# A list schedule for the engine order, a permutation product for the slot exponentials, and token sums in the experts' mask

## The chip, the cores and the metric

The kernel runs on one core of a Trainium2 chip. The metric is the device time of one execution in microseconds, median of several runs; the profile is one execution of its own, with a span from its first to its last instruction and a somewhat longer measured time. The core has TensorE (PE, with a separate row PEld for its weight loads), VectorE (DVE), ScalarE (ACT), GpSimd (POOL, which here issues the input loads and makes a few constants) and SyncE (SP, which issues the output stores). Each engine works through its own instructions in order.

## The reference

Two stages. The first is causal attention for 4 batches, 8 heads, 768 positions and head dimension 64. Heads marked as retrieval see all earlier positions; the others see the first 4 positions and a window of 64. The result, as 3072 rows of 512, goes into a soft mixture of experts with 8 experts of 4 slots each:

```python
    scores = scale * np.matmul(q, k.transpose(0, 1, 3, 2))
    ...
    stream_keep = causal & (is_sink | in_win)
    ...
    a = np.exp(scores)
    a = a / (np.sum(a, axis=-1, keepdims=True) + 1e-09)
    return np.matmul(a, v).astype(np.float32)
...
    logits = x @ phi
    d = np.exp(logits - logits.max(0)); d /= d.sum(0) + 1e-09
    slot_input = (d.T @ x).reshape(E, S_per_e, D)
    for e in range(E):
        h = np.maximum(slot_input[e] @ w1[e], 0.0)
        slot_out[e] = h @ w2[e]
    c = np.exp(logits - logits.max(1)); c /= c.sum(1) + 1e-09
    return (c @ slot_out).astype(np.float32)
```

(The lines of the second part are shortened; x is the attention's result, w1 is 512 x 1024 for each expert, w2 is 1024 x 512.) The two softmaxes of the second part share their exponentials: one is divided by a sum over tokens for each slot, the other by a sum over slots for each token.

## The kernel before

**Units.** A unit of attention is a pair of heads, number n of 16; two pairs make a quad Q, four pairs a batch b. All matmul operands are bf16; the loads convert from f32. A raw quad of q, k or v holds 16 consecutive tokens in one partition, so that one load is a few long runs. In this layout a block of 128 tokens is a permutation of the natural order.

**One quad's turns.** `turn_half` (L79; `turn_pair`, L90, for quad 0, which arrives in two pieces) transposes half of a quad's q, k or v by 16 TensorE transposes into a PSUM buffer of the pool "tr" (two buffers, L57), and `copy` (L104) brings it to SBUF, by VectorE ("V") or ScalarE ("A"). `turn_back` (L110) transposes v once more into the rows that the second product reads. ScalarE takes the second half of k and of v; VectorE the rest.

**One pair.** `qk` (L134) makes the scores of the causal triangle in six groups of 448 columns for both heads, each into one of two PSUM buffers of the pool "sc" (L55), and ScalarE's exponential (L142) writes each group to pT. `mask` (L145) multiplies parts of pT by 0/1 masks on VectorE; `make_vfar` (L121) makes a masked copy of v for blocks far from the diagonal; `pvmm` (L163) makes the products with v, with a column of ones for the row sums, in one PSUM buffer; `norm` (L175) divides, on VectorE, into xb. `x_transpose` (L186) turns xb through "tr" into xT.

**One batch.** `logits` (L195) multiplies xT by phi in "tr", and ScalarE's exponential (L206) writes el, four times repeated over 128 columns. `exp_slots` (L208) transposes el through "tr", and ScalarE copies it to expT (L214), which is kept for the end, with its sum over tokens in colpart. The copy puts the tokens into natural order by its output pattern: element s of a run of 16 comes 16 elements, 32 bytes, behind its neighbour in the loop that writes. `dispatch` (L230) sums el times xb for the batch in "tr" and adds it to slot_acc (L240). `row_sums` (L221) makes the sums over slots from expT.

**Order.** The loop over n (L404) writes out by hand which group goes to each engine's queue and where: scores of pair n, products of pair n-1 between them, the turns of the next quad as four `tasks`, and the slot work of the last full batch in the four pairs behind it. A PSUM group and the instruction that empties it are issued side by side.

**Loads.** POOL issues them in program order: q, k, v of the next quad but one when the present quad has been turned, the 16 weight loads of 1 MB (as bf16) in between. Their SBUF tiles for w2 of experts 4 to 7 are first used as the raw buffers and the masks, so these loads come last.

**End.** Behind the loop stand the logits of the last batch, `exp_slots`, `dispatch`, the sum over tokens (csum, L510), its reciprocal (rcol, L512), and the scaling of slot_acc to slot_sc (L516). Then sip (L523), its copy siT (L524), two groups of hp against w1 (L535), the relu and mask hs (L539 on ScalarE, L540 on VectorE; emask, made at L399, is 1 where a row belongs to the expert), `second` against w2 (L557), and the output rows with their stores (L582 to L600).

Of the kernel before, what the change touches and what calls it, by code (L numbers as in the profile page):

```python
# [21 lines left out]
UNIT = 448  # L22
# [15 lines left out]

class Attn:
# [3 lines left out]
    def __init__(self, nc, tc, ctx, sctx, src, env):  # L43
# [16 lines left out]
        self.lg, self.el = {}, {}  # L60
# [20 lines left out]
    def turn_half(self, t, Q, hf, eng):  # L81
        raw = self.raws[t][Q % 2]
        tp = self.trp.tile([128, 8, 96], BF16, tag="tr", name="tp" + t)
        for s in range(8):
            d0 = (8 * hf + s) * 64
            for hp in range(2):
                self.nc.tensor.transpose(tp[64 * hp:64 * hp + 64, s, :], raw[:96, hp, d0:d0 + 64],  # L87
                                         self.ident[:96, :96])
        dst = self.blocked(t, Q).rearrange("c g (s p) -> c s g p", p=8)[:, 8 * hf:8 * hf + 8]
        self.copy(eng, dst, tp.rearrange("c s (g p) -> c s g p", p=8))  # L90

    def turn_pair(self, t, a, eng):
        raw = self.raws[t][0]
        p0 = 64 * a
        tp = self.trp.tile([128, 16, 48], BF16, tag="tr", name="tp" + t)
        for s in range(16):
            for hp in range(2):
                self.nc.tensor.transpose(tp[64 * hp:64 * hp + 64, s, :],  # L98
                                         raw[p0:p0 + 48, hp, s * 64:s * 64 + 64],
                                         self.ident[p0:p0 + 48, p0:p0 + 48])  # L100
        dst = self.blocked(t, 0).rearrange("c g (s p) -> c s g p", p=8)[:, :, 6 * a:6 * a + 6]
        self.copy(eng, dst, tp.rearrange("c s (g p) -> c s g p", p=8))

    def copy(self, eng, o, i):  # L104
        if eng == "A":
            self.nc.scalar.copy(o, i)  # L106
        else:
            self.nc.vector.tensor_copy(o, i)  # L108

    def turn_back(self, Q, a, eng):  # L110
        tp = self.trp.tile([128, 6, 2, 64], BF16, tag="tr", name="tpb")
        vT = self.vT[Q]
        for i in range(6):
            self.nc.tensor.transpose(tp[:, i].rearrange("p h d -> p (h d)"), vT[:, 6 * a + i, :],  # L114
                                     self.ident)
        self.copy(eng, self.vbs[Q % 2][:, a, :, :, :64].rearrange("p h j d -> p j h d"), tp)
# [13 lines left out]
    def qk(self, n, u):  # L130
# [4 lines left out]
        for j, q0, o, w in unit_pieces(u):  # L135
            for hh in range(2):
                ps = slice(64 * hh, 64 * hh + 64)
                nc.tensor.matmul(sc[:, hh, o:o + w], kT[ps, (g0 + j) * 128:(g0 + j + 1) * 128],  # L138
                                 qT[ps, g0 * 128 + q0:g0 * 128 + q0 + w], start=True, stop=True)
        if u == 0:  # L140
            self.pT[n] = self.ptp.tile([128, 2, NPT], BF16, tag="pT", name="pT")
        nc.scalar.activation(self.pT[n][:, :, u * UNIT:(u + 1) * UNIT], sc[:, :, :UNIT], ACT.Exp,  # L142
                             scale=self.scale)
# [41 lines left out]
    def x_transpose(self, n):  # L185
# [7 lines left out]
        self.nc.vector.tensor_copy(self.xT[b][:, n4], tp)  # L193

    def logits(self, b, i0, i1):  # L195
# [7 lines left out]
        if i1 == 6:  # L203
            self.el[b] = self.small.tile([128, 6, 4, 32], BF16, tag="el", name="el")
            lg = self.lg[b].rearrange("p i (o s) -> p i o s", o=1)
            nc.scalar.activation(self.el[b], lg.to_broadcast([128, 6, 4, 32]), ACT.Exp)  # L206

    def exp_slots(self, b):  # L208
        nc = self.nc
        tp = self.trp.tile([128, 768], BF16, tag="tr", name="tpe")  # L210
        for i in range(6):
            nc.tensor.transpose(tp[:, i * 128:(i + 1) * 128],  # L212
                                self.el[b][:, i].rearrange("p g s -> p (g s)"), self.ident)
        nc.scalar.activation(self.expT[:, b, :].rearrange("g (i p s) -> g i s p", i=6, p=8),  # L214
                             tp.rearrange("g (i s p) -> g i s p", i=6, p=8), ACT.Copy,
                             accum_out=self.colpart[:, b:b + 1])
# [4 lines left out]
    def row_sums(self, b):  # L221
# [6 lines left out]
        self.nc.vector.reciprocal(self.rrow[:, b, :], rp)  # L228

    def dispatch(self, b):  # L230
        nc = self.nc
        sp = self.trp.tile([128, 512], F32, tag="tr", name="slp")
        for i in range(6):
            g = i % 4
            nc.tensor.matmul(sp[32 * g:32 * (g + 1), :], self.el[b][:, i, 0, :], self.xb[b][:, i, :],
                             start=(i < 4), stop=(i + 4 >= 6))
        if b == 0:
            nc.vector.tensor_copy(self.slot_acc, sp)
        else:
            nc.vector.tensor_add(self.slot_acc, self.slot_acc, sp)  # L240
# [3 lines left out]
def kernel(  # L244
# [34 lines left out]
    phi = singles.tile([P, 4, ES], BF16, name="phi")  # L279
    quarter = singles.tile([P, 1], BF16, name="quarter")  # L280
# [15 lines left out]
    tkf = singles.tile([P, 2], F32, name="tkf")  # L296
# [9 lines left out]
    def w2_half(e, c):  # L306
# [6 lines left out]
               slot_acc=slot_acc, msk=msk, fmask=fmask, scale=1.0 / (D ** 0.5), raws=raws, vbs=vbs)  # L313
# [7 lines left out]
    with tc.tile_pool(name="setup", bufs=1) as setup:  # L321
# [21 lines left out]
        for vb in vbs:  # L343
            nc.vector.memset(vb, 1.0)
        nc.vector.tensor_single_scalar(ident, iti, 0.0, op=ALU.is_equal)
        at.turn_pair("q", 0, "V")
        at.turn_pair("k", 0, "A")
# [6 lines left out]
        nc.vector.tensor_single_scalar(tkf[:, 1:2], tkf[:, 0:1], float(n_sink), op=ALU.is_lt)  # L354
        causal = setup.tile([P, 256], BF16, name="causal")
# [16 lines left out]
    head_mask(0)  # L372
    head_mask(2)
# [3 lines left out]
    def weights(c):  # L377
        for _ in range(c):
# [8 lines left out]
    weights(1)  # L387

    def setup_sums():
        nc.gpsimd.tensor_copy(phi, phf)  # L390
        nc.gpsimd.memset(sum4, 1.0)
        for g in range(4):
            nc.gpsimd.affine_select(sum4[32 * g:32 * (g + 1)], sum4[32 * g:32 * (g + 1)],
                                    pattern=[[-1, ES]], compare_op=ALU.is_equal,
                                    fill=0.0, base=0, channel_multiplier=1)
        for e4 in range(2):
            for g in range(4):
                s0 = SPE * (4 * e4 + g)
                nc.vector.reduce_sum(emask[32 * g:32 * (g + 1), e4:e4 + 1],  # L399
                                     sum4[32 * g:32 * (g + 1), s0:s0 + SPE], axis=AX.X)  # L400

    NWQ = [1, 1, 2, 1, 2, 1]
    none = lambda: None

    for n in range(NP + 1):
        last = n == NP
        Q = n // 2
        tasks = []
        if n == 0:
            tasks = [lambda: at.turn_pair("v", 0, "V"), lambda: at.turn_back(0, 0, "V"),  # L410
                     lambda: at.turn_pair("q", 1, "V"), lambda: at.turn_pair("k", 1, "A")]
        elif n % 2 == 1 and Q + 1 < NQ:
            tasks = [lambda: at.turn_half("q", Q + 1, 0, "V"), lambda: at.turn_half("k", Q + 1, 0, "V"),
                     lambda: at.turn_half("q", Q + 1, 1, "V"), lambda: at.turn_half("k", Q + 1, 1, "A")]
            if n == 1:
                tasks += [lambda: at.turn_pair("v", 1, "V"), lambda: at.turn_back(0, 1, "V")]
        elif n % 2 == 0 and not last:
            tasks = [lambda: at.turn_half("v", Q, 0, "V"), lambda: at.turn_half("v", Q, 1, "A"),
                     lambda: at.turn_back(Q, 0, "V"), lambda: at.turn_back(Q, 1, "V")]
        tasks += [none] * 6  # L420

        def loads():
            if n % 2 == 0 and Q + 2 < NQ:
# [3 lines left out]
            elif n % 2 == 1 and Q + 2 < NQ:  # L427
                at.load("v", Q + 2)
                weights(NWQ[Q] - 1)

        if Q > 0:
            loads()
        if n == 1:
            setup_sums()
        if n == 12:
            weights(12 - wi[0])
        if n == 15:
            w_load(NE + 4)
            w_load(NE + 5)

        b = (n - 5) // 4
        bt = (n - 5) % 4 if n >= 5 else None

        def qk(u):
            if not last:
                at.qk(n, u)

        qk(0)
        tasks[0]()
        if bt == 0:  # L450
            at.logits(b, 0, 3)
        qk(1)
        if n:
            for i in range(5):
                at.pvmm(n - 1, 0, i)
        if bt == 0:
            at.logits(b, 3, 6)
        qk(2)
        if n:
            at.pvmm(n - 1, 0, 5)  # L460
            for i in range(3):
                at.pvmm(n - 1, 1, i)
        if not last:
            at.mask(n, 0, 4)
        qk(3)
        if n:
            for i in range(3, 6):
                at.pvmm(n - 1, 1, i)
            at.norm(n - 1)
        if bt == 0:  # L470
            at.exp_slots(b)
        tasks[1]()
        qk(4)
        tasks[2]()
        if not last:
            at.mask(n, 1, 3)
        if bt == 1:
            at.dispatch(b)
        qk(5)
        tasks[3]()  # L480
        if n:
            at.x_transpose(n - 1)
        if not last:
# [164 lines left out]
```

## Time and profile before

| | |
|---|---|
| median of 3 runs | 198.06 us (197.72 to 199.22) |
| profiled execution: time, span | 196.88 us, 195.2 us |
| mean granted TensorE clock | 0.847 of full speed |
| PE busy, share of the span | 141.5 us, 72% |
| PEld | 93.8 us, 48% |
| VectorE | 117.1 us, 60% |
| ScalarE | 125.4 us, 64% |
| POOL | 30.6 us, 16% |
| POOL's DMA queue | 26.22 MB, its packets took 73.2% of 16 engines' span |
| stage: before the first exponential | 0 to 8.7 us |
| stage: attention loop, first to last exponential | 8.7 to 145.7 us |
| stage: last products to siT | 145.7 to 159.4 us |
| stage: experts and output rows | 159.4 to 186.5 us |
| stage: last stores landing | 186.5 to 195.2 us |

The groups of a page list busy time, the mean of one instruction, and the idle time of its engine just before it with what ended that idle time. A busy TensorE is not one at its peak: at half the granted clock the same work shows as more busy time. In a timeline the duration belongs to the merged run of instructions.

### The profile page before, as it was taken

Reading aid. Unit: us, or ns where it says so; the run is one execution under the profiler, and the core shown is the slowest. Engines: PE = TensorE matmul, PEld = TensorE weight load, DVE = VectorE, ACT = ScalarE, POOL = GpSimd, SP = SyncE. Lnnn points to the kernel's source line nnn. Section 1 sums busy time; section 2 is a strip of 40 time slices with the busy share of each in tenths; the row PEclk is TensorE's granted clock in tenths of the full one; section 3 lists DMA queues with packets and bytes.
Section 4 is the critical chain, followed back from the end, with each engine's and each line's share of the span. In section 5 each row is a group of like instructions: output and inputs, shape, how many; then the busy total and the mean of one; then the engine's idle time right before and its main releaser. Section 6 shows DMA issues by size and latency. Waiting matters only on the chain. (4 is left out here: it accounts for less than half of the span.)

```text
span 195.2 us, 5613 instructions
## 1 busy us (share of the span) xinstructions
PE 141.5 (72%) x2508; PEld 93.8 (48%) x2508; DVE 117.1 (60%) x247; ACT 125.4 (64%) x148; POOL 30.6 (16%) x58
## 2 busy tenths in 40 slices
PE   7888888878939788893997889479674536688500
PEld 2455655655726465672654666346354212475100
DVE  6679987987544769654648867464865222136600
ACT  3376848789896777979765887976670531318620
POOL 7615051032012103200322000021031000000000
PEclk9955969999985999998569999966997558999965
DMA  4999999999989954999799997049969900008997
GB/s 65 169 194 224 202 226 200 225 201 222 212 181 138 220 107 77 200 213 188 113 222 205 212 215 151 3 64 217 187 81 149 168 1 3 0 3 265 342 405 278
DMA packets 16087, 32.93 MB, mean 169 GB/s; under 512 B 1728, under 2 KB 8896, under 8 KB 14272
## 3 DMA queue, kind: packets, MB, share of 16 engines
q0 software_dynamic: 11216, 26.22, 73.2%
q1 hardware_dynamic: 4848, 6.37, 9.3%
q8 instruction: 19, 0.31, 0.6%
q14 instruction: 4, 0.03, 0.0%
HBM read 52.50 MB, written 6.29 MB: 301 GB/s over the span
## 5 line engine op out<-in xcount | busy, mean ns | idle before, releaser
L142 ACT ACTIVATE pT<-sc 128x896 bf16<-128x896 f32 x96 | 86.2, 926 | 27.0 <-PE sc L138 22.9
L161 DVE TENSOR_TENSOR pT<-pT,w 128x1024 bf16<-128x1024 bf16 (+1 forms) x64 | 31.8, 518 | 23.5 <-ACT pT L142 23.5
L138 PE MATMUL sc<-qT,kT 64*128 64x128 bf16 (+4 forms) x352 | 39.5, 302 | 3.3 <-ACT kT L106 2.5
L170 PEld LDWEIGHTS <-pT 128*128 128x128 bf16 x672 | 27.5, 105 | 16.3 <-issue 16.2
L170 PE MATMUL pv<-vf,pT 128*128 128x65 bf16 x320 | 27.1, 205 | 5.0 <-DVE vf L125 4.9
L170 PE MATMUL pv<-vb,pT 128*128 128x65 bf16 x352 | 30.4, 205 | 0.0
L87 PEld LDWEIGHTS <-w 96*64 96x64 bf16 x672 | 20.2, 121 | 19.2 <-issue 18.2
L138 PEld LDWEIGHTS <-kT 64*128 64x128 bf16 x352 | 11.4, 98 | 13.0 <-ACT kT L106 4.1
L182 DVE TENSOR_TENSOR xb<-pv,rs 128x768 bf16<-128x768 f32 x16 | 15.3, 957 | 0.6
L87 PE MATMUL tpq<-ident,w 96*64 96x96 bf16 x224 | 8.2, 220 | 10.2 <-ACT expT L214 9.1
L108 DVE COPY qT<-tpq 128x768 bf16<-128x768 bf16 x16 | 8.8, 552 | 10.3 <-PE tpq L87 7.6
L214 ACT ACTIVATE expT<-tpe 128x768 bf16<-128x768 bf16 x4 | 13.6, 3399 | 0.9 <-PE tpe L212 0.9
L191 PE MATMUL tpx<-ident,xb 128*128 128x128 bf16 x96 | 9.3, 242 | 3.7 <-DVE xb L182 2.0
L114 PE MATMUL tpb<-ident,vT 128*128 128x128 bf16 x96 | 8.4, 226 | 4.6 <-ACT vT L106 4.0
L108 DVE COPY vb<-tpb 128x768 bf16<-128x768 bf16 x16 | 8.9, 554 | 4.9 <-PE tpb L114 4.9
L68 POOL DMA_DIRECT2D w<-in_q_dram x7 | 4.5, 645 | 43.3 <-PE tpq L87 21.8
L125 DVE TENSOR_TENSOR vf<-vb,fmask 128x528 bf16<-128x528 bf16 x16 | 11.1, 695 | 0.0
L193 DVE COPY xT<-tpx 128x768 bf16<-128x768 bf16 x16 | 8.9, 555 | 3.4 <-PE tpx L191 3.0
L106 ACT COPY kT<-tpk 128x768 bf16<-128x768 bf16 x9 | 7.2, 797 | 5.4 <-PE tpk L98 5.2
L114 PEld LDWEIGHTS <-vT 128*128 128x128 bf16 x96 | 5.6, 100 | 8.3 <-ACT vT L106 5.9
L87 PE MATMUL tpk<-ident,w 96*64 96x96 bf16 x224 | 8.1, 219 | 1.9 <-DVE kT L108 1.9
L191 PEld LDWEIGHTS <-xb 128*128 128x128 bf16 x96 | 6.8, 107 | 5.1 <-DVE xb L182 2.4
(89 smaller groups left out, 164.2 us busy)
## 6 DMA issues: line engine op xcount, KB each, us to landing
w<-in_moe_w_dram POOLq DMA_DIRECT2D x14, 1024.0 KB, 13.2
out_dram<-ot SPq DMA_DIRECT2D x12, 256.0 KB, 3.1
out_dram<-ot SPq DMA_DIRECT2D x6, 512.0 KB, 4.9
w<-in_q_dram POOLq DMA_DIRECT2D x7, 384.0 KB, 6.7
w<-in_k_dram POOLq DMA_DIRECT2D x7, 384.0 KB, 7.2
w<-in_v_dram POOLq DMA_DIRECT2D x7, 384.0 KB, 8.9
w<-in_moe_w_dram POOLq DMA_DIRECT2D x4, 512.0 KB, 9.3
w<-in_q_dram POOLq DMA_DIRECT2D x2, 192.0 KB, 5.4
```

What stands on the lines that cost most here:

```text
L87: self.nc.tensor.transpose(tp[64 * hp:64 * hp + 64, s, :], raw[:96, hp, d0:d0 + 64], self.ident[:96, :96])
L108: self.nc.vector.tensor_copy(o, i)
L114: self.nc.tensor.transpose(tp[:, i].rearrange("p h d -> p (h d)"), vT[:, 6 * a + i, :], self.ident)
L125: self.nc.vector.tensor_mul(vf, self.vbs[n // 2 % 2][:, n % 2, :, :4, :], fm.to_broadcast([128, 2, 4, VW]))
L138: nc.tensor.matmul(sc[:, hh, o:o + w], kT[ps, (g0 + j) * 128:(g0 + j + 1) * 128], qT[ps, g0 * 128 + q0:g0 * 128 + q0 + w], start=True, sto ...
L142: nc.scalar.activation(self.pT[n][:, :, u * UNIT:(u + 1) * UNIT], sc[:, :, :UNIT], ACT.Exp, scale=self.scale)
L161: nc.vector.tensor_mul(v, v, m)
L170: self.nc.tensor.matmul(pv[:, hh, i * 65:(i + 1) * 65], pT[:, hh, o:o + 128], (vb if i - j <= 1 else vf)[:, j, :65], start=(j == 0), stop= ...
L182: nc.vector.tensor_mul(x, pv[:, :, :, :64], rs.to_broadcast([128, 2, 6, 64]))
L191: self.nc.tensor.transpose(tp[:, i * 128:(i + 1) * 128], self.xb[b][:, i, n4 * 128:(n4 + 1) * 128], self.ident)
L193: self.nc.vector.tensor_copy(self.xT[b][:, n4], tp)
L214: nc.scalar.activation(self.expT[:, b, :].rearrange("g (i p s) -> g i s p", i=6, p=8), tp.rearrange("g (i s p) -> g i s p", i=6, p=8), ACT ...
```

## The change

1. **Order.** The handwritten loop is replaced by a class `Plan`. It lists every group of instructions as an operation with an engine, a cost, a delay until others see its result, what it depends on, a rank (place in the order of pairs plus an offset by kind), and, for PSUM users, the pool. `order` is a list schedule: it keeps a time for each engine, and takes again and again the operation that could start first; on one engine, among those that could start within `lead`, the lowest rank. TensorE pays 0.115 for a change of row groups. The instructions are then issued in that order. Each PSUM group and the copy that empties it are operations of their own, so the functions are split (`turn`/`turned`, `back`/`blocked_back`, `qk`/`exp`, `x_transpose`/`x_transposed`, and so on). All v turns are copied by VectorE; ScalarE keeps the second half of k.
2. **Slot exponentials.** The transposes in `exp_slots` become matmuls of el with a permutation matrix `perm`, into an "sc" buffer in f32; ScalarE copies it in natural order without a stride.
3. **Token sums.** slot_sc is now slot_acc plus the last batch's dispatch, added directly and not scaled; the reciprocal of the token sums scales emask, which the relu applies. emask's sums move from pair 1 to the end.
4. **Small ones.** Only the last two columns of the v tiles are set to ones; head masks 1 and 3 are made before the loop; weight loads are spread as 1, 1, 1, 1, 1, 2 with the rest behind the turn of v of quad 6 and w2 of experts 4, 5 behind that of quad 7.

The core of the diff:

```diff
+    def turn(self, t, Q, h, deps, rank, at=0.0, cost=0.33):
+        n = f"{t}{Q}.{h}"
+        back = t == "b"
+        self.add("T" + n, "PE", cost, 0.27, deps, rank, "T", mode="F" if back else "C", slot=("tr", "e" + n), at=at)
+        eng = self.evac.get(n, self.evac.get(f"{t}{h}", "DVE"))
+        c, d = (0.68, 0.85) if eng == "ACT" else (0.464, 0.6)
+        self.add("e" + n, eng, c, d, ["T" + n], rank, "eT")
...
+                add(f"Q{n}.{u}", "PE", 0.19, 0.27, d, n + u / 6, "Q", mode="H", slot=("sc", f"x{n}.{u}"))
+                d = [f"Q{n}.{u}"] + ([f"P{n - 2}.1.B"] if u == 0 and n > 1 else [])
+                add(f"x{n}.{u}", "ACT", 0.814, 0.95, d, n + u / 6, "x")
...
+            for h in range(2):
+                d = [f"Tb{Q - 1}.1"]
+                self.turn("v", Q, h, d, n + 1 + h / 4, at=8.0 if Q == 1 else 0.0)
...
+                add(f"G{b}", "PE", 0.35, 0.27, [f"el{b}"], n + 0.4, "G", slot=("sc", f"eG{b}"))
+                add(f"eG{b}", "ACT", 1.2, 1.35, [f"G{b}"], n + 0.5, "eG")
...
+                    st = max(r, free[e])
+                    key = (st if st > free[e] + lead else free[e], o["rank"])
+                    if top is None or key < top[0]:
+                        top = (key, st + (SWITCH if e == "PE" and o["mode"] != mode else 0.0), o)
...
+RANK = {"D": -0.22, "V": 1.15, "x": 2.77, "M": -1.62, "eX": 0.07, "eD": 0.79, "M5": -0.31, "eT": -0.45,
+        "X": 0.66, "P": 0.44, "G": 0.12, "el": -0.31, "L": -0.76, "H": -0.26, "N": -0.18, "eG": 0.8,
+        "T": -0.79}
+EVAC = {"k1": "ACT"}
+LEAD = 0.1
...
     def exp_slots(self, b):
-        tp = self.trp.tile([128, 768], BF16, tag="tr", name="tpe")
+        tp = self.scp.tile([128, 2, 512], F32, tag="sc", name="tpe")
         for i in range(6):
-            nc.tensor.transpose(tp[:, i * 128:(i + 1) * 128],
-                                self.el[b][:, i].rearrange("p g s -> p (g s)"), self.ident)
-        nc.scalar.activation(self.expT[:, b, :].rearrange("g (i p s) -> g i s p", i=6, p=8),
-                             tp.rearrange("g (i s p) -> g i s p", i=6, p=8), ACT.Copy,
-                             accum_out=self.colpart[:, b:b + 1])
+            o = 128 * (i % 3)
+            self.nc.tensor.matmul(tp[:, i // 3, o:o + 128], self.el[b][:, i].rearrange("p g s -> p (g s)"),
+                                  self.perm, start=True, stop=True)
+        self.tp["g", b, 0] = tp
+
+    def exp_slots_out(self, b):
+        self.nc.scalar.activation(self.expT[:, b, :].rearrange("g (a c) -> g a c", a=2),
+                                  self.tp.pop(("g", b, 0))[:, :, :384], ACT.Copy,
+                                  accum_out=self.colpart[:, b:b + 1])
...
-            nc.vector.memset(vb, 1.0)
+            nc.vector.memset(vb[:, :, :, :, 64:], 1.0)
...
+        nc.vector.tensor_tensor(tkf[:, 2:3], tkf[:, 0:1], tk[:, 0:1], op=ALU.subtract)
+        nc.vector.tensor_scalar(perm, iti, tkf[:, 2:3], None, op0=ALU.is_equal)
...
-    head_mask(0)
-    head_mask(2)
+    for h in (0, 2, 1, 3):
+        head_mask(h)
...
+    def after_turn(t, Q):
+        turned.add((t, Q))
+        if Q + 2 < NQ:
+            if t == "v":
+                at.load("v", Q + 2)
+                weights(NWQ[Q] - 1)
+            elif ("q", Q) in turned and ("k", Q) in turned:
+                at.load("q", Q + 2)
+                at.load("k", Q + 2)
+                weights(1)
+        elif t == "v" and Q == NQ - 2:
+            weights(12)
+        elif t == "v":
+            for e in (4, 5):
+                w_load(NE + e)
...
+    at.dispatch(bl)
+    slp = at.tp.pop(("d", bl, 0))
+        nc.vector.tensor_add(slot_sc[:, cs].rearrange("p (h a d) -> p a h d", h=2, a=2),
+                             pair(slot_acc), pair(slp))
     at.exp_slots(bl)
-    at.dispatch(bl)
+    at.exp_slots_out(bl)
+    for e4 in range(2):
+        for g in range(4):
+            s0 = SPE * (4 * e4 + g)
+            nc.vector.reduce_sum(emask[32 * g:32 * (g + 1), e4:e4 + 1],
+                                 sum4[32 * g:32 * (g + 1), s0:s0 + SPE], axis=AX.X)
     csum = at.small.tile([P, 1], F32, tag="cs", name="csum")
     nc.vector.reduce_sum(csum, colpart, axis=AX.X)
     rcol = at.small.tile([P, 1], F32, tag="rc", name="rcol")
     nc.vector.reciprocal(rcol, csum)
-        nc.vector.tensor_scalar_mul(slot_sc[:, cs].rearrange("p (h a d) -> p a h d", h=2, a=2),
-                                    slot_acc[:, cs].rearrange("p (a h d) -> p a h d", h=2, a=2), rcol)
+    nc.vector.tensor_scalar_mul(emask, emask, rcol)
```

## The prediction

> **What bounds the kernel now.** I read the page first, then the exponentials of ScalarE in order of time (one pair of heads is six of them), then TensorE in order of time around the odd gap, then a table of stretches, and last the chain of waits for the end of the kernel.
>
> The page, groups of instructions (busy us, mean ns | idle before, releaser):
>
> ```profile
> L142 ACT ACTIVATE pT<-sc 128x896 bf16<-128x896 f32 x96 | 86.2, 926 | 27.0 <-PE sc L138 22.9
> L87 PE MATMUL tpq<-ident,w 96*64 96x96 bf16 x224 | 8.2, 220 | 10.2 <-ACT expT L214 9.1
> L214 ACT ACTIVATE expT<-tpe 128x768 bf16<-128x768 bf16 x4 | 13.6, 3399 | 0.9 <-PE tpe L212 0.9
> ```
>
> The attention loop runs from the first exponential at 8.71 us to the last one's end at 145.71: 137.0 us, in which ScalarE is idle 27.0 us, mostly for scores. One instruction stands out: the slot copy, 3.40 us, four times.
>
> TensorE in order of time (start, duration, [idle before]):
>
> ```profile
> 52.84 0.53 PE L87 MATMUL tpk<-ident,w 96*64 96x96 bf16 x16
> 53.31 0.37 PE L138 MATMUL sc<-qT,kT 64*128 64x256 bf16 x4
> 56.72 0.64 PE L87 MATMUL tpq<-ident,w 96*64 96x96 bf16 x16 [3.04 <-ACT expT L214]
> 57.29 0.56 PE L138 MATMUL sc<-qT,kT 64*128 64x320 bf16 x4
> 57.77 0.85 PE L87 MATMUL tpk<-ident,w 96*64 96x96 bf16 x16
> ```
>
> TensorE stands 3.04 us because the slot transposes hold one of the two "tr" buffers until the slow copy ends; afterwards the same 16 transposes take 0.85 us, not 0.53. The table of stretches (PE, PEld, DVE, ACT, POOL busy; PEclk; DMA share; GB/s) says why:
>
> ```profile
> 34.00:57.00 23.00, 17.20 (x382) 12.49 (x383) 16.86 (x36) 19.85 (x22) 3.02 (x5) 1.00 1.08 216
> 57.00:64.00 7.00, 6.83 (x97) 4.28 (x91) 3.55 (x8) 4.76 (x6) 1.83 (x3) 0.51 0.86 138
> 64.00:92.00 28.00, 21.27 (x452) 15.20 (x452) 19.39 (x39) 23.31 (x26) 3.66 (x6) 0.98 0.87 168
> 92.00:101.00 9.00, 8.83 (x129) 5.95 (x125) 4.87 (x10) 5.65 (x8) 1.83 (x3) 0.50 0.83 148
> ```
>
> After this wait and its two repetitions (before 91.59 and 127.41, 3.04 us each) the granted clock is 0.50 to 0.54 for 7 to 9 us; elsewhere in the loop from 34 us it is about 1.0.
>
> The chain of waits, at the end (start, duration):
>
> ```profile
> 153.36 0.84 PE tpe L212 x6
> 154.22 3.42 ACT expT L214 x2
> ...
> 158.06 0.63 DVE slot_sc L516 x2
> 158.69 0.05 issue
> 158.73 0.33 PE sip L523 x4
> 159.06 0.02 issue
> 159.08 0.30 DVE siT L524
> ```
>
> Here the fourth copy lies on the path itself. The sum below is made on the span of 195.2 us; the profiled run took 196.88 us, the median of the runs is 198.06, so 2.9 us is added to a span.
>
> **Part 1, the slot copy in the loop.** Starts of the first exponential give the periods of pairs 3 to 14: 7.92, 6.47, 11.90, 8.97, 7.67, 6.33, 12.11, 9.71, 7.67, 6.33, 11.60, 9.46. Undisturbed, an odd pair takes 7.67 and an even one 6.38. Pairs 5, 9, 13 hold the copy: excess 4.23 + 4.44 + 3.93 = 12.6. Pairs 6, 10, 14 hold the half clock: 2.59 + 3.33 + 3.08 = 9.0. Sum 21.6 us. What stays, three times: the exponential of the logits (0.71 us, from its start at 50.96 to the next start at 51.67) and a copy that writes in order. The nearest row for that copy is L206, 128x768 from f32 PSUM, 0.81 us; the accumulator read (0.50 us) overlaps the old copy, so between 0.81 and 1.31: I take 1.2. That is 3 x 1.95 = 5.85. **Gain 15.7 us** (21.6 if the stays fit in ScalarE's idle time; 12.6 - 5.85 = 6.7 if the half clock has another cause than the wait). The product with the permutation is 6 matmuls for 6 transposes, nothing on TensorE. It takes a "sc" buffer: for about 0.4 + 1.2 us the scores have one buffer, so ScalarE may wait one score group (0.30 us) once or twice, up to 1.8 us in three rounds, against the same time freed in "tr"; inside the bound above.
>
> The Trainium skill speaks against the half of this. TensorE: Matmul & The Clock Gate, "What's actually happening", says that the clock falls after a whole idle window of about 3.4 us; 3.04 us would not fill it. By that rule the 9.0 us would have another cause and stay, and the sum below would be 179.2. I go by the rows: three waits of 3.04 us, three falls of the clock directly behind them, and no wait of that length and no fall elsewhere from 34 to 128 us.
>
> **Part 2, the order.** At full clock the three engines have, per pair, from start to start in the timeline: ScalarE 6 exponentials at 0.845 (3.38 for four in a row), one kT copy per two pairs (0.70), slot work 0.49: 5.9. The seven vT copies leave it for VectorE. VectorE: masks 0.60 + 0.60 + 0.53, vf 0.62, norm 1.13, xT 0.47, 3.5 turned copies at 0.47, slot work 0.18: 5.8. TensorE: scores 6 x 0.30 (46.70 to 47.00), pv 1.35 (15 matmuls in 0.48, so 42), turns (6 x 0.46 + 2 x 0.44)/2 = 1.82, x 0.43, slot work (0.92 + 0.42 + 0.55 + 0.16)/4 = 0.51: 5.9. So nothing in the loop can be below 5.9 per pair, and the order of before, with the slot work that stays, makes (7.67 + 6.38)/2 + 0.49 = 7.5. The odd pairs carry four q and k turns and no room for them; spreading these is what a list order can win. Three engines at the same load leave no slack for in-order queues: I take 6.6, nearer the middle than the floor. 12 pairs x 0.9 = **11.0 us gain**; floor 5.9 gives 19.4, the old spacing 0. Pairs 0 to 2 (7.9, 9.6, 7.6; half clock until 18.6 us) I leave, as their clock does not come from the order.
>
> **Small edits.** Two more head masks (1 and 3) stand before the loop: 4 x 0.42 = 1.7 us on VectorE ahead of the first vT copy at 10.78; VectorE is idle 0.3 to 0.9 us at a time there: cost 0.8, between 0 and 1.7. The ones of vb shrink (2 x 1.38 us at 1.5 to 4.5 us), but TensorE runs its zeros until 5.63 and the identity is ready at 4.63: nothing; without the zeros it would be 2.5. Two tiny setup operations, 0.35 us, replace the 1.27 us of emask sums, which go to the end. The loads move on POOL's queue: 26.22 MB at about 215 GB/s are 122 us in all. By the sum below the last exponential ends at 145.7 - 15.7 - 11.0 + 0.8 = 119.8. Four weights (1 MB, 4.9 us each) are issued behind v's turn of quad 6 (about 2 pairs of 6.6 earlier than the last turn), w2 of experts 4 and 5 behind v's turn of quad 7, which is ranked 2.8 pairs before the end (about 101 us), the halves of 6 and 7 behind the last mask (about 121). Four halves of 2.4 us land near 131; second() for experts 6 and 7 begins 13.6 us behind siT (as in the chain of before), near 145. Hidden by 14 us.
>
> **Part 3, the end.** From the end of the exponential of the logits (153.31) to the end of siT (159.38) are 6.07 us. After: dispatch 1.04 (its row at the half clock), two adds from PSUM, about 0.45 each (an estimate from the 0.69 us of the whole add), so the sums are ready at +2.0. TensorE's permutation, 0.82 behind dispatch, is done at +1.9, the copy of 1.2 at +3.2. On VectorE, eight emask sums (1.27 us) stand in the queue, then csum, which waits for the copy, then rcol and the scaling, and behind them siT, which all of hp waits for. csum and rcol follow each other by 0.19 and 0.20 us in the chain of before; so csum starts at 3.2, rcol at 3.4, the scaling at 3.6, siT at 3.8 and ends at +4.1. sip itself is done at +2.4 and is covered. **Gain 2.0 us** (1.0 to 3.6, the latter if nothing stood ahead of siT). The first hp group runs cold (3.59 us against 1.87) and stays so: TensorE is idle here in both. From there the 35.8 us to the end are not changed.
>
> Sum: -15.7 - 11.0 + 0.8 - 2.0 = -27.9; 195.2 - 27.9 = 167.3 span, 198.06 - 27.9 = **170.2 us**.
>
> **Rivals.** (a) The order wins nothing: TensorE's real group times differ from the plan's (it has 0.33 us for 16 transposes, the rows 0.46 start to start, with a separate charge of 0.115 for a change of mode), so a fixed order stalls where the old one did. Then -15.7 + 0.8 - 2.0: 181.2. For it: the three loads are equal. Against: odd pairs at 7.67 with even ones at 6.38 show unevenness that any spreading removes.
> (b) Slower: the clock does not come back. At the half clock a pair costs TensorE 6 x 0.49 + 2.63 (15 pv matmuls in 0.94) + 3.1 (16 transposes in 0.79) + 0.76 + 0.9 (slot work) = 10.4 us; 13 such pairs, from 33.9 us on, and the 49.5 us behind the last exponential, less 2.0, give a span of 33.9 + 135 + 47.5 = 216, or 219 us. It decides from 8.7 us per pair, that is when more than 55% of the pairs run cold. For it: between 22 and 26 us TensorE is idle only 0.39 to 0.65 us at a time, busy 63%, and the clock is 0.57 behind. Against: at 6.6 per pair it would be busy 90%.
> (c) The copy does not get faster: if f32 PSUM or the accumulator made the 3.40 us and not the stride of 32 bytes at the output, part 1 is lost, part 2 halved, and part 3 about zero: 193 us. Against: L206 reads f32 PSUM of the same size in 0.81 us.
>
> **Numbers.** The forecast (both parts) 0.74, 161 to 177; (a) 0.18, 177 to 184; (b) 0.04, 200 and above; (c) 0.04, 188 to 196. The low end 161 is the floor of 5.9 per pair (170.2 - 8.4 = 161.8) with a little of the bound of part 1. The range 161 to 182 leaves out (b), (c) and the upper part of (a). Within 1% is what this measurement can't tell from no change. Half of (c) falls within 1% if its order wins less still. Faster by over 1%: 0.74 + 0.18 + 0.02 = 0.94; same 0.02 from (c); slower 0.04 from (b).
>
> **What would show it.** Part 1: the expT row near 1 us, no 3 us wait of TensorE, PEclk about 1.0 from pair 3 to 15. Part 2: pairs of equal length near 6.6, ScalarE about 90% busy in the loop, the last exponential ending near 120 us. Part 3: the end of siT about 4.1 us behind the exponential of the logits, csum in the chain. Wrong if the PEclk row has fives inside the loop, if "sc" or "tr" waits of 2 us or more come up in TensorE's queue, or if the pairs stay above 7.5.

## The result and the profile after

The changed kernel takes 164.06 us (median of 4 runs, 162.0 to 166.7) against 198.64 us in the same comparison, 34.6 us less; the forecast was 27.9 us less. The ratio is 0.818, with a 95% interval of 0.808 to 0.828. Executions of one kernel spread by 1 to 5 us with the mean clock (0.899 at a span of 160.3 us, 0.862 at 165.0), so every ratio here leaves the slow ones out, and the rows of four profiles below are an upper end (v's copies on ScalarE, both moves of masks, the second set at the start: 2 to 4 us above their fastest). The profiled execution has a span of 160.3 us, 34.9 us less than before. The spans by stage, from the timelines of the two kernels:

| stage | before | after | difference | forecast |
|---|---|---|---|---|
| start to the first exponential of pair 3 | 33.9 | 35.2 | +1.3 | +0.8 |
| pairs 3 to 15, to the end of the last exponential | 111.8 | 79.5 | -32.3 | -26.7 |
| to the end of the last exponential of the logits | 7.6 | 6.0 | -1.6 | 0 |
| from there to the first hp product | 6.1 | 3.7 | -2.4 | -2.0 |
| to the end | 35.8 | 35.8 | 0.0 | 0 |

The page of the changed kernel, groups of instructions (busy us, mean ns, then idle before and its releaser):

```profile
L283 ACT ACTIVATE pT<-sc 128x896 bf16<-128x896 f32 x96 | 81.6, 922 | 9.6 <-PE sc L276 7.8
L302 DVE TENSOR_TENSOR pT<-pT,w 128x1024 bf16<-128x1024 bf16 (+1 forms) x64 | 32.1, 519 | 3.3 <-ACT pT L283 2.7
```

ScalarE waits 9.6 us ahead of its exponentials, where it was 27.0, and VectorE 3.3 us ahead of its masks, where it was 23.5. One exponential is not faster (922 ns, 926 before).

ScalarE in order of time in the changed kernel, around the first slot copy (start, duration):

```profile
54.41 0.81 ACT L362 ACTIVATE expT<-tpe 128x768 bf16<-128x768 f32 x1
55.12 0.19 ACT L362 ACTIVATION_READ_ACCUMULATOR expT<-tpe 128x1 f32 x1
55.21 0.91 ACT L283 ACTIVATE pT<-sc 128x896 bf16<-128x896 f32 x1
```

The copy is 0.81 us in place of 3.40, and from its start to the next exponential it takes 0.80 us: nothing of the accumulator read stands on the path.

The table of stretches of the changed kernel (PE, PEld, DVE, ACT, POOL busy; PEclk; DMA share; GB/s):

```profile
11.20:23.60 12.40, 9.58 (x166) 6.68 (x166) 10.83 (x25) 6.79 (x9) 4.22 (x8) 0.50 1.09 212
36.00:57.00 21.00, 20.45 (x457) 15.05 (x451) 20.50 (x43) 19.64 (x26) 3.11 (x5) 1.00 1.08 212
57.00:78.00 21.00, 19.64 (x449) 14.42 (x444) 19.56 (x41) 19.64 (x24) 7.10 (x12) 1.00 1.08 213
78.00:100.00 22.00, 20.83 (x470) 14.81 (x467) 20.87 (x43) 20.30 (x27) 2.49 (x4) 1.00 1.04 216
```

From 36 to 100 us TensorE, VectorE and ScalarE are each busy 92% or more at the full clock, and no half clock follows a slot copy in the loop. The DMA engines are full too, at 212 to 216 GB/s, where there were holes before. The first row is the weak place: pair 0 takes 12.4 us at the half clock.

The chain of the changed kernel at its end (start, duration):

```profile
119.96 0.82 ACT el L351
120.82 0.79 PE slp L385 x6
121.64 0.75 DVE slot_sc L634 x2
...
124.48 3.63 PE hp L665 x32
```

### The profile page after: what moved, and what is told of

Read it like the earlier page. It is cut to its first block, busy times and chain, and to the rows that moved or that the text cites. A ratio compares the mean times of both kernels' runs of the same rounds, so it can differ in the third digit from the quotient of the medians.

```text
span 160.3 us, 5605 instructions
## 1 busy us (share of the span) xinstructions
PE 127.5 (80%) x2506; PEld 87.9 (55%) x2508; DVE 117.1 (73%) x256; ACT 107.4 (67%) x141; POOL 30.6 (19%) x58
## 4 chain that ended last, share of the span: by engine, by line
PE 50%; DVE 25%; ACT 16%; issue 3%
ACT pT L283 11%; PE sc L276 11%; PE pv L311 9%; DVE pT L302 5%; DVE xb L323 5%; PE tpv L228 3%; PE hp L665 3%; PE tpk L228 3%; PE tpx L332 3%; PE tpq L228 3%; PE zp L494 3%; PE sp L687 3%; DVE w L527 2%; PE tpb L248 2%; ACT ot L731 2%
## 5 line engine op out<-in xcount | busy, mean ns | idle before, releaser
L283 ACT ACTIVATE pT<-sc 128x896 bf16<-128x896 f32 x96 | 81.6, 922 | 9.6 <-PE sc L276 7.8
L276 PE MATMUL sc<-qT,kT 64*128 64x128 bf16 (+4 forms) x352 | 34.2, 281 | 1.1 <-ACT pT L283 0.6
L311 PEld LDWEIGHTS <-pT 128*128 128x128 bf16 x672 | 25.1, 97 | 10.1 <-issue 7.8
L311 PE MATMUL pv<-vb,pT 128*128 128x65 bf16 x352 | 28.7, 193 | 1.2 <-DVE xb L323 1.1
L228 PEld LDWEIGHTS <-w 96*64 96x64 bf16 (+1 forms) x864 | 22.7, 121 | 9.4 <-issue 5.9
L311 PE MATMUL pv<-vf,pT 128*128 128x65 bf16 x320 | 24.4, 194 | 0.3 <-issue 0.3
L208 POOL DMA_DIRECT2D w<-in_q_dram x7 | 4.6, 657 | 35.8 <-PE sc L276 31.9
L228 PE MATMUL tpk<-ident,w 96*64 96x96 bf16 (+1 forms) x288 | 9.9, 216 | 1.2 <-DMA w<-in_k_dram 0.9
L228 PE MATMUL tpv<-ident,w 96*64 96x96 bf16 (+1 forms) x288 | 9.4, 219 | 1.4 <-issue 1.3
L228 PE MATMUL tpq<-ident,w 96*64 96x96 bf16 (+1 forms) x288 | 9.8, 216 | 0.4 <-DMA w<-in_q_dram 0.4
L242 DVE COPY vT<-tpv 128x768 bf16<-128x768 bf16 x16 | 8.4, 552 | 1.5 <-PE tpv L228 1.4
```

The costliest lines, as they stand in the source:

```text
L228: self.nc.tensor.transpose(tp[64 * hp:64 * hp + 64, x, :], raw[p0:p0 + rows, hp, s * 64:s * 64 + 64], self.ident[p0:p0 + rows, p0:p0 + rows])
L283: self.nc.scalar.activation(self.pT[n][:, :, u * UNIT:(u + 1) * UNIT], self.sc.pop((n, u))[:, :, :UNIT], ACT.Exp, scale=self.scale)
L311: self.nc.tensor.matmul(pv[:, hh, i * 65:(i + 1) * 65], pT[:, hh, o:o + 128], (vb if i - j <= 1 else vf)[:, j, :65], start=(j == 0), stop= ...
```

## The experiments

Each was timed beside the kernel before on one chip. The ratio is that to the kernel before, with its 95% interval; spans and rows are of its one profile. "From pair 3" is the time from pair 3's first exponential to the end of the last one: 111.8 us before, 79.5 after.

**Old order, new copy.** In the kernel before:

```diff
-        tp = self.trp.tile([128, 768], BF16, tag="tr", name="tpe")
+        tp = self.scp.tile([128, 2, 512], F32, tag="sc", name="tpe")
...
-            nc.tensor.transpose(tp[:, i * 128:(i + 1) * 128],
-                                self.el[b][:, i].rearrange("p g s -> p (g s)"), self.ident)
+            self.nc.tensor.matmul(tp[:, i // 3, o:o + 128], self.el[b][:, i].rearrange("p g s -> p (g s)"),
+                                  self.perm, start=True, stop=True)
```

> The kernel before with the slot copy of the change alone: permutation product into f32 of pool sc, copy without stride; the order of before. My theory (the copy's 3.40 us costs its own time and the clock behind it): the excess of pairs 5, 9, 13 (12.6 us) and of 6, 10, 14 (9.0 us) falls to what stays, 3 x (0.71 + 0.80) = 4.5, so 17 us less in the loop, 2.4 us less at the end: about 179 us, and granted clock near 1.0 in the loop. Rival 1 (the clock falls for another cause): pairs 6, 10, 14 keep 9.0 us, about 188 us. Rival 2 (all of the gain is the order): above 195 us.

Measured: 182.1 us, ratio 0.919 (0.913 to 0.925), span 180.3. From pair 3: 96.7 us, 15.1 less. Pairs 5, 6, 9, 10 take 8.7, 7.5, 8.7, 7.5 us where they took 11.9, 9.0, 12.1, 9.7. The stretches say that the clock goes too (same columns as above):

```profile
34.00:57.00 23.00, 19.07 (x414) 13.72 (x412) 18.95 (x40) 19.43 (x24) 4.58 (x8) 1.00 1.07 210
57.00:64.00 7.00, 5.83 (x116) 3.77 (x115) 5.12 (x11) 5.88 (x7) 0.92 (x2) 1.00 1.07 212
```

The second row had 0.51 in the kernel before. So part 1 is 15 us in the loop, and neither rival holds. The edit does two things, though: it shortens the copy, and it moves the buffer that the copy holds from "tr" to "sc". What each is worth by itself in the old order was not separated. At the end nothing was gained in this profile: siT is done 4.2 us behind the exponential of the logits (6.1 before), but both hp groups run at the half clock (3.60 and 3.33 us, 3.56 and 1.91 before), and from the last exponential to the end it is 49.4 us in both kernels.

**Old order, the wait filled.** In the kernel before, ahead of the transposes that wait:

```diff
         qk(4)
+        if bt == 0:
+            at.fill(n - 1, 32)
```

`fill` issues 32 products of the identity with itself, 112 columns each, into unused columns of pv.

> The kernel before with 32 products of the identity with itself (112 columns each, into unused columns of pv, about 2 us at full clock), in TensorE's queue ahead of the transposes that wait for the slow copy. The wait itself stays. My theory (the idle 3.04 us lowers the clock): clock stays near 1.0 in pairs 6, 10, 14 and 9 us go: about 190 us. Rival 1 (another cause): pairs 6, 10, 14 stay near 9.0 to 9.7 us and the time at 198 to 199. Rival 3 (the products come on the path): 200 or more.

Measured: 194.34 us, ratio 0.981 (0.974 to 0.988); from pair 3 107.5 us. TensorE in order of time:

```profile
54.70 1.73 PE L197 MATMUL pv<-ident 128*128 128x112 bf16 x32 [0.82 <-DVE xb L182]
56.97 0.53 PE L87 MATMUL tpq<-ident,w 96*64 96x96 bf16 x16 [0.54 <-ACT expT L219]
57.43 0.37 PE L138 MATMUL sc<-qT,kT 64*128 64x320 bf16 x4
57.73 0.53 PE L87 MATMUL tpk<-ident,w 96*64 96x96 bf16 x16
```

The transposes wait for the copy until 56.97 as before, but behind it they run in 0.53 us, not 0.85, and the clock from 57 to 64 us is 1.00; so it is in the second round. In these two rounds, then, it was TensorE's idleness that lowered the clock, not the copy. In the third round the clock falls although the wait is filled in the same way (stretches, same columns):

```profile
97.00:122.60 25.60, 21.25 (x436) 15.48 (x437) 18.03 (x37) 21.07 (x25) 1.84 (x4) 1.00 0.86 179
122.60:130.00 7.40, 6.36 (x114) 4.42 (x113) 4.00 (x8) 5.75 (x9) 1.06 (x2) 0.77 0.71 125
```

TensorE's rows behind the fill are at full speed there until 125.7 us, then slow (16 transposes in 0.85 us); two waits of 0.52 and 0.80 us stand ahead of the fall, and the other two rounds have nearly the same waits without one. Why this round differs is open. The size was half of what I expected, 4.3 us of the 9.0: pairs 6 and 10 fall to 7.5 us, not to 6.4, and pair 14 only from 9.5 to 8.9. The 1.1 us that stay in pairs 6 and 10 are work: the dispatch and row sums of the batch, which I had put down to the clock.

**List order, strided copy.** In the changed kernel the identity takes the place of the permutation, out of one f32 buffer in "sc", and the copy's output has the old stride:

```diff
-                                  self.perm, start=True, stop=True)
+                                  self.ident, start=True, stop=True)
...
-        self.nc.scalar.activation(self.expT[:, b, :].rearrange("g (a c) -> g a c", a=2),
+        self.nc.scalar.activation(self.expT[:, b, :].rearrange("g (i p s) -> g i s p", i=6, p=8),
```

> The changed kernel with the identity in place of the permutation, so that the copy has to put the tokens in order by its strided output again, out of f32 PSUM in pool sc. Everything else is the list order. If the stride makes the 3.40 us, the copy's row is 3.4 us again; then, if ScalarE bounds the loop, 3 x 2.6 us more there and 2.6 at the end: 164 + 10 = 174; if the clock falls behind it as in the order before, up to 9 us more: 183. Rival (c) of the prediction (f32 PSUM or the accumulator made it slow): copy 0.8 us and 164. If the list order hides the copy: below 169.

Measured: 172.55 us, ratio 0.868 (0.859 to 0.877), span 169.7, 9.4 more than the changed kernel: 6.0 from pair 3, 2.4 at the end, 1.0 at the start. ScalarE in order of time:

```profile
55.50 3.44 ACT L361 ACTIVATE expT<-tpe 128x768 bf16<-128x768 f32 x1
58.45 0.49 ACT L361 ACTIVATION_READ_ACCUMULATOR expT<-tpe 128x1 f32 x1
58.47 3.62 ACT L283 ACTIVATE pT<-sc 128x896 bf16<-128x896 f32 x4
```

With f32 PSUM and the accumulator the same, only the output's stride makes 3.44 out of 0.81 us. Rival (c) falls. And the list order hides much of what the old one could not: the copy's buffer is in "sc", the turns go on, and TensorE waits for the three copies of the loop 1.53, 1.12 and 2.11 us, not 3.04. Behind the first two the clock stays at 1.00; behind the third it is 0.51 from 113 to 120 us, and pair 15 takes 6.4 us in place of 5.0.

**List order without its offsets.**

```diff
-    plan = Plan(RANK, EVAC, LEAD, NP)
+    plan = Plan({}, EVAC, LEAD, NP)
```

> The changed kernel with all offsets of RANK at zero: still a list schedule with the same costs and dependencies, but ties go by pair number alone. If the offsets carry the gain of the order: pairs of 7 us or more in place of 6.1, 164 + 10 to 14 = 174 to 178. If any list schedule is as good: 163 to 167.

Measured: 172.34 us, ratio 0.871 (0.864 to 0.878), span 170.6. From pair 3: 87.6 us. So of the 17.2 us from 96.7 to 79.5, a plain list schedule gives 9.1, and the offsets by kind the other 8.1.

**v's copies, once in each order.** In the changed kernel back to ScalarE, and in the old order (with the new copy) over to VectorE:

```diff
-EVAC = {"k1": "ACT"}
+EVAC = {"k1": "ACT", "v1": "ACT"}
```

> The changed kernel with the second half of v's turns copied by ScalarE again (EVAC with v1), order made anew by the same list schedule. If the three engines are level in the loop, as the prediction counted, ScalarE gets 0.35 us per pair more (0.70 for one of two pairs) and is the bound: pairs 6.1 to 6.45, 13 x 0.35 = 4.5 us more, about 168. If VectorE was the bound, the loop gets shorter, 161.

```diff
-            tasks = [lambda: at.turn_half("v", Q, 0, "V"), lambda: at.turn_half("v", Q, 1, "A"),
+            tasks = [lambda: at.turn_half("v", Q, 0, "V"), lambda: at.turn_half("v", Q, 1, "V"),
```

> As old_order_new_copy (hand-written order, new slot copy), and all of v's turns copied by VectorE, as the changed kernel has it. If the change of engine carries a part of the order's gain of 17 us by itself: 3 to 5 us less, 177 to 179. If it is worth something only together with the order, since ScalarE is not the bound of the old order: 181 to 183; more if VectorE's later masks delay the products.

Measured: 174.18 us, ratio 0.871 (0.858 to 0.885), for the first. From pair 3 83.9 us, 4.4 more, as expected from level engines. Another 7.1 us, which I did not expect, are ahead of pair 3, which begins at 42.3 us (the clock is 0.50 from 9 to 40 us but for 3.4 us of it), and 2.2 behind the loop. For the second: 188.85 us, ratio 0.952 (0.944 to 0.959), 6.7 us slower than with ScalarE's copies. In its list of waits (waiter, released by: us in total, times, longest):

```profile
ACT pT L142 <- PE sc L138: 29.5, 46, 1.7
...
PE tpb L114 <- DVE vT L108: 9.4, 9, 1.2
```

The old order places the turn back directly behind v's turn, and VectorE is not free there: TensorE waits 9.4 us for vT (4.8 with ScalarE's copies), and ScalarE 29.5 us for scores (16.9). My expectation of no change was wrong: from pair 3 on, the same move costs 3.8 us in one order (100.5 against 96.7) and saves 4.4 in the other.

**siT first, and TensorE's waits at the end filled.** In the changed kernel emask's sums, csum, rcol and the scaling go behind siT; the second run also fills waits, with eleven products of 512 columns at four places, of which one is shown:

```diff
+    at.fill(w1s[0], 1)
     nc.vector.tensor_copy(siT, sip)
+    for e4 in range(2):
+        for g in range(4):
...
+    nc.vector.tensor_scalar_mul(emask, emask, rcol)
```

> The changed kernel with siT issued on VectorE ahead of emask's sums, csum, rcol and the scaling. In the changed kernel sip is ready at 122.76 and siT waits for VectorE until 124.14. If siT's place in the queue costs that: 1.3 us less, hp from 123.1, about 162.7. Rival: emask comes too late for hs: no gain, 164.

> As list_siT_first, and 11 products of the identity with w1 (512 columns, into an unused sc buffer) fill TensorE's waits between the last products and hp. If TensorE's idle time there lowers the clock: first group of hp 1.9 us in place of 3.6, 1.7 us less again, about 161. If not: 162.7, and more if the products come on the path (up to 2 us).

Measured: 163.33 us, 0.813 (0.802 to 0.824), and 159.65 us, 0.803 (0.792 to 0.813). The first can't be told from 0.818 by time; its rows show hp 2.60 us behind the dispatch, 3.66 in the changed kernel. TensorE in order of time in the second:

```profile
121.81 0.61 PE L392 MATMUL slp<-xb,el 128*32 128x512 bf16 x6 [0.24 <-ACT el L358]
122.35 0.51 PE L364 MATMUL tpe<-perm,el 128*128 128x128 bf16 x6
123.27 0.31 PE L650 MATMUL sip<-sum,slot_sc 128*128 128x32 bf16 x4 [0.41 <-DVE slot_sc L643]
123.96 1.91 PE L673 MATMUL hp<-w,siT 128*32 128x512 bf16 x32 [0.39 <-DVE siT L652]
```

hp is 1.91 us in place of 3.63. From the dispatch to the first product of `second` are 10.4 us (121.81 to 132.22), 13.6 in the changed kernel and 12.6 with siT first alone, so the fill is worth 2.2 us. The stage ahead of the dispatch is as long as in the changed kernel (6.1 us from the last exponential's end in both).

**Head masks later.** In the changed kernel two of the four head masks ahead of the loop, and the plan's own, go to later places among the first pairs:

```diff
-    for h in (0, 2, 1, 3):
-        head_mask(h)
+    head_mask(0)
+    head_mask(2)
...
+    later = {"M0.13": (1, 3), "M0.5": (4, 6), "eb1.1": (5, 7)}
```

> The changed kernel with only head masks 0 and 2 ahead of the loop; 1 and 3 behind the second mask of pair 0, 4 and 6 behind its last, 5 and 7 behind quad 1's second back turn; the plan's own mask operations are not issued at their place. In the changed kernel ten of sixteen mask instructions (4.08 us) stand ahead of the first vT copy at 13.42, and ScalarE waits from 12.16 to 16.56. If this wait is theirs: first vT copy near 11.1, pair 3 begins about 2 us earlier, 162. If the half clock of the first 23 us or the loads set the pace: 164.

Measured: 166.56 us, 0.838 (0.829 to 0.848): slower. The second exponential starts 2.4 us earlier (14.15 against 16.56), but pair 3 begins at 36.9, not 35.2: the masks now stand ahead of the first vf, the first products wait 0.98 us for it, and the half clock lasts until 28 us. Another 2.5 us are lost from pair 3 on (82.0) and 1.8 behind the loop, for which I have no cause.

**The start filled.** On top of the filled tail, in the wait ahead of the first back turn, and then also among the turns behind it:

```diff
+        at.fill_start({"Tb0.0": 6}.get(name, 0))
```

> As list_tail_filled, and six products of the identity with qT (512 columns each, into pv's buffer before its first use) in TensorE's queue ahead of quad 0's first back turn, where it waits 2.8 us for VectorE (11.2 to 14.0 us in the changed kernel). In the changed kernel the granted clock is 0.50 from 9 to 24 us although TensorE's row is full from 14 us on. If dense products bring the clock back: about 1.0 from 14 us on, pair 3 begins at 31 to 33 us in place of 35.2, about 157. If the clock stays (transposes of 48 rows don't hold it): no change, 159.7. If they come on the path: 160 to 162.

> As list_start_filled, with six more such products among the next turns (one ahead of k's second turn, two ahead of v's second, two ahead of q's first of quad 1, one ahead of the second back turn), up to 2.6 us on TensorE's path at half clock. If a single burst is lost again in the run of transposes, this holds the clock: 156 to 158. If the first burst alone does it, or none does: 160 to 162.

Measured: 157.91 us, 0.795 (0.790 to 0.800), and 158.55 us, 0.797 (0.791 to 0.803). By time neither is clear of the filled tail alone, 0.803 (0.792 to 0.813); the rows say more. Pair 3 begins at 32.7 and 33.7 us. The changed kernel, the strided copy, siT first and the filled tail, which have one and the same order up to there, have it at 34.8 to 36.2. TensorE in order of time in the first run, then a stretch of it, then the changed kernel's row for the same turns:

```profile
11.40 2.74 PE L350 MATMUL pv<-qT,ident 128*128 128x512 bf16 x6
...
14.96 0.69 PE L228 MATMUL tpk<-ident,w 48*64 48x48 bf16 x32
```

```profile
16.00:20.00 4.00, 3.37 (x95) 2.44 (x94) 4.00 (x10) 3.80 (x6) 1.78 (x3) 1.00 1.07 222
```

```profile
14.77 1.05 PE L228 MATMUL tpk<-ident,w 48*64 48x48 bf16 x32
```

Ahead of the burst of 2.74 us the turns of this profile take 1.05 us, as at the half clock of the changed kernel; behind it they take 0.69. So the clock comes back behind the burst, by 14.1 us, where the changed kernel has it back at 25.6. (The clock column of this profile has 1.00 ahead of 14 us too, and that of the strided copy ahead of 27.8 us; the durations of the rows there don't bear it out.) In the second run it is back at 15.7 us, and its further products gain nothing. But the burst alone is no guarantee: the next run has the same one, and its clock stays at 0.50. The first has the lowest time of all versions, 157.91 us.

**Masks on POOL.** On top of list_start_filled, the masks of heads 4 to 7:

```diff
+    for h in (4, 6, 5, 7):
+        for c, r in ((0, r0), (256, r1)):
+            nc.gpsimd.tensor_scalar(msk[:, h, c:c + 256], delta, r[:, h:h + 1], None, op0=ALU.mult)
+            nc.gpsimd.tensor_tensor(msk[:, h, c:c + 256], msk[:, h, c:c + 256], stream, op=ALU.add)
```

> As list_start_filled, and the masks of heads 4 to 7 are made by POOL (a product and a sum for each half, 16 instructions) instead of eight instructions of VectorE among the first pairs. In list_start_filled VectorE is full from 8 to 24 us (3.85 to 4.00 of each 4 us). If its 3.3 us of masks are on the path there: pair 3 begins up to 3 us earlier, 155. If POOL's instructions hold up its DMA issues or VectorE: 158 or more.

Measured: 166.25 us, 0.837 (0.831 to 0.842), 8 us worse. Its stretches, behind the burst at the start:

```profile
13.00:18.00 5.00, 4.49 (x79) 2.80 (x79) 2.60 (x6) 1.52 (x3) 4.75 (x7) 0.50 0.68 126
18.00:23.00 5.00, 5.00 (x87) 3.45 (x84) 3.58 (x7) 3.64 (x5) 4.75 (x6) 0.50 0.01 3
```

The clock comes back only at 25.8 us. POOL is full for 14 us with 16 instructions of 0.66 to 1.43 us, its DMA issues stand behind them, and the DMA engines fall to 3 GB/s. Pair 2 takes 12.8 us, since the turns of quad 2 wait 4.4 us for q. Whether a shorter form on POOL would do was not tried.

## Why the prediction was right, and where its sizes were off

**Part 1, right.** Forecast -15.7 in the loop; alone it gave -15.1 from pair 3. What stays was put at 1.95 us per batch (0.71 + 1.2 are 1.91, a slip of 0.1 us in all), with 1.2 for the copy; the copy is 0.80. In its place there was work that I had counted as clock: of the 9.0 us of pairs 6, 10 and 14, about 1.1 us per batch is the dispatch and row sums. The two errors nearly cancel, which is luck. The skill's rule that I weighed (TensorE: Matmul & The Clock Gate, "What's actually happening") asks for a whole idle window of about 3.4 us. The runs ask for less: the clock fell behind all three waits of 3.04 us, behind one of 2.11 us in the list order with the strided copy, and behind none of the filled waits but the third; with the new copy, without such a wait, it did not fall in the loop. Here the measurement decides.

**Part 2, right in kind, too small.** This is the term that carries the miss (5.6 of 7.0 us): 12 pairs x 0.9 = 11.0 us, from an assumed 6.6 us per pair. The changed kernel takes 74.5 us for these 12 pairs, 6.2 each, against the floor of 5.9 that the prediction counted, and the order gave 17.2 us (96.7 to 79.5) beyond the copy. I took the middle because three level engines leave in-order queues no slack. The runs show that the offsets by kind buy just this: without them the 12 pairs take 81.8 us, 6.8 each, near my 6.6. Moving v's copies to VectorE is no gain by itself; it costs in the old order and pays in the list order, presumably because there TensorE has other work meanwhile.

The two parts are also not a plain sum. With the order first and the copy last, the copy is worth 9.4 us (169.7 to 160.3); with the copy first it is worth 14.9 (195.2 to 180.3): the old order turns it into three stops of TensorE of 3.04 us with the half clock behind each, the list order into shorter ones with one half clock.

**Small edits.** Forecast +0.8 (0 to 1.7), found +1.3. I counted two more head masks ahead of the first vT copy. In truth ten mask instructions stand there, 4.08 us, as the plan puts the first of its own masks (two instructions) at its time zero, when it takes VectorE as idle, and there the setup still runs. That these masks make up the 1.3 us isn't shown: with some of them moved, pair 3 began no earlier, and between four profiles of this same start it moves by 1.4 us, so that +0.8 and +1.3 can't be told apart. The loads had 14 us of cover by the forecast; the last ones were issued at 115.9 us and the DMA engines are full until about 130, and the first products of `second` begin at 134.4, so they stayed hidden.

**Part 3, right in size, but not by the wait that I named.** Forecast -2.0, found -2.4. VectorE's queue holds siT, as described, but csum does not wait for the copy. VectorE in order of time in the changed kernel:

```profile
122.31 1.27 DVE L641 TENSOR_REDUCE emask<-sum 32x1 f32<-32x4 bf16 x8
123.61 0.16 DVE L644 TENSOR_REDUCE csum<-colpart 128x1 f32<-128x4 f32 x1
123.80 0.16 DVE L646 RECIPROCAL rcol<-csum 128x1 f32<-128x1 f32 x1
124.00 0.23 DVE L647 TENSOR_SCALAR emask<-emask,rcol 128x2 f32<-128x2 f32 x1
124.14 0.28 DVE L654 CAST siT<-sip 128x128 bf16<-128x128 f32 x1
```

The copy and its accumulator read are done at 123.3, and csum starts at 123.61, directly behind emask's sums: with a copy of 0.81 us, not 1.2, these sums are the longer branch. sip was done at 122.76, so the queue costs 1.4 us, and siT ends 3.7 us behind the exponential of the logits, not 4.1. hp stayed cold (3.63 us), as forecast. The 1.6 us between the last exponential and the logits were not in the forecast: the plan makes vf ahead of the last masks, and the last products no longer wait 1.58 us for it.

**The rivals.** (a), an order that wins nothing, is refuted by 96.7 against 79.5 us. (b), a clock that does not come back, holds only for the start, where it was also before; behind 26 us the loop is at 1.00. (c) is refuted by the strided copy.

## What to carry to other kernels

When one slow instruction holds a buffer, cost the stop of the engine that waits for it, and what its clock does afterwards, beside the instruction's own time; then ask whether a mere reorder would hide it. In this loop with level engines the floor per step (a gain of 19.4 us) was a better forecast for a tuned list schedule than a value near the middle (11.0; 17.2 measured), but the schedule's view of the start is worth checking against the setup that runs ahead of it. Products that compute nothing, put where TensorE waits anyway, were worth about 2 us at the end and, by the rows, 1 to 3 at the start, where their effect on the clock was not the same in every run.

## What the runs showed of the hardware

A ScalarE write of bf16 with a stride of 32 bytes took 3.40 us for 768 elements, 0.81 without. The Trainium skill has the cause that fits, in SBUF — State Buffer (its note on SBUF "cachelines"): lines of 16 bytes, with a penalty for each access that goes to a new line; it gives no size for ScalarE, and these rows do. No other stride was run. The accumulator read behind the same copy shows 0.50 us after the strided one and 0.19 after the other.

The granted clock stayed at 0.50 from 14 to 24 us in the changed kernel with TensorE's row full, while it ran transposes of 48, 96 and 128 rows and some scores; with six products of 512 columns ahead of the same sequence it was back at 14.1 us in one profile and at 15.7 in another, but only at 25.8 in a third. So a full row did not bring the clock back there; which property of the instructions counts was not separated. In every trace the clock keeps a value for a multiple of 3.41 us (3.41, 6.83, 10.24 and so on, the last stretch aside), so it may matter how a burst or a wait falls against these steps; no run varies that.

VectorE's mask instruction took 0.41 us on average in the run of ten in the changed kernel (4.08 us), and 0.58 in the run of eight while POOL made the other masks. VectorE's copies out of PSUM next to them take 0.54 to 0.56 us in both. That POOL's work slows VectorE's masks is a likely reading, but only this one pair of rows stands behind it.
